# Filling TensorE's waits in a prologue with matmuls that nothing reads

## The chip, the cores and the metric

The kernel runs on one core of one Trainium2 chip. The metric is the device time of one execution in microseconds (us), lower is better. An execution has one launch; the arithmetic is all on the chip.

## The reference

A sliding-window attention is followed by a gated two-layer network. The attention has 8 batches of 576 tokens, 8 heads of 64 dimensions, and each token sees itself and the 63 before it. Its output, 4608 tokens by 512, goes through the network.

```python
scores = (1 / sqrt(64)) * q @ k.T            # rel = i - j, kept where 0 <= rel < 64
attn = softmax(scores) ; x = attn @ v        # x: 4608 x 512
h = x @ w_in                                 # w_in: 512 x 2048
g = h * erf(log(1 + exp(h)))
out = g @ w_out                              # w_out: 2048 x 512, float32
```

The weights arrive as 64-bit floats and have to be brought to the chip's formats by the kernel itself.

## The kernel before

All large products run on TensorE in 16-bit floats, each operand split into a high and a low part, so that a product is three matmuls (high by high, high by low, low by high). Every operand is first scaled by a power of two that its own maximum gives.

The program has two stages that overlap. In the prologue, up to roughly 190 us, the 16 pieces of the 64-bit weights are fetched (L, line 472), turned into 32-bit floats by shifts and masks on VectorE with help of ScalarE and GpSimd (g, d, dd, c, o), and their maxima taken (b, line 508). For each pair of pieces TensorE turns the column of maxima into a row (mb, line 514), VectorE takes its top (mx, line 517), TensorE spreads the top over 128 partitions (my, line 520), and VectorE makes the exponent and the scale from it (mc, lines 305 and 308). ScalarE writes a scaled diagonal (dg, line 529). Then the high part is a scaled copy (h), and the low part is a sum on TensorE: an fp32 matmul of the raw piece with the diagonal, minus the high part (lp, lines 551 and 552), copied out by ScalarE or VectorE (le, line 442 on VectorE). The scales of a chunk of 256 tokens go the same way: row of maxima (pb, line 351), top (px, line 355), spread (py, line 359), copy and scale (pc, line 362).

Attention works on tiles of 128 tokens: scores (s, line 392), masked maximum (m), exponentials on ScalarE, a transposing DMA, weighting of the values (a, line 425), division (n). The network works on chunks of 256 tokens and halves of its 2048 columns: first layer (mm, line 588) into hp, gate on ScalarE and VectorE, second layer (mA and mB, line 624) into o. Attention of later tiles runs beside the network of earlier ones, and after the prologue TensorE has work nearly all the time.

The order of all of it is one long table of words, PLAN (line 47): each word is a step with its arguments, and a loop at the end calls the steps in that order. Each engine executes its own instructions in this order and waits, by semaphores, only for what a step needs. Nothing overtakes on an engine, apart from loads of weights on TensorE.

One tile in TensorE's accumulation memory, av (line 280), holds two banks of 512 columns: the weighted values in the first columns of each, then the rows and columns of the scale steps just described (crow, call, wrow, wall, lines 283 and 284). The columns from 391 on of the first bank are unused. The identity matrix ident (128x128, bf16) is made by GpSimd at the start (line 292).

Of the kernel before, what the change touches and what calls it, by code (L numbers as in the profile page):

```python
# [19 lines left out]
W = 64  # L20
DM, DF = 512, 2048
NT = B * S
P = 128
# [189 lines left out]
def window_attention_gated_ffn(ctx, tc, q, k, v, w_in, w_out, masks, out):  # L213
    nc = tc.nc
# [420 lines left out]
    def store(c, j):  # L635
        r0 = c * CT + j * P
        nc.sync.dma_start(out[r0:r0 + P, :], ob[c % len(ob)][:, j, :])

    def table(n):
        nc.scalar.preload_act_table_set(("exp_and_others", "softplus", "sigmoid_and_others")[n])  # L640

# [64 lines left out]
```

## Time and profile before

| What | Value |
|---|---|
| Median of 3 runs | 949.46 us (947.31 to 952.27) |
| The profiled execution | 949.97 us |
| its span in the profile | 948.2 us |
| TensorE busy (matmuls) | 882.9 us, 93% |
| VectorE, ScalarE, GpSimd busy | 688.1, 639.1, 306.1 us |
| Mean granted clock as recorded | 0.986 |

PE is TensorE's matmuls and PEld its loads of weights, DVE is VectorE, ACT ScalarE, POOL GpSimd, SP the engine that issues the DMAs. A row such as "L551 MATMUL o<-stage,diag x2" names the line of the kernel, the result and the operands. The idle time in brackets is that of the engine just before the row, and behind the arrow stands what ended it. An fp32 matmul shows as two records. A granted clock of 1.00 is 2.4 GHz and 0.50 is 1.2 GHz, its two levels; a value between is a mean over the stretch.

### The profile page before, as it was taken

What the parts mean: (1) busy time and instruction counts of PE and PEld (TensorE: products, weight loads), DVE (VectorE), ACT (ScalarE), POOL (GpSimd) and SP (SyncE); (2) the same over time, 40 slices, a digit from 0 to 9 for tenths busy, and PEclk for the clock granted to TensorE, in tenths of its full rate; (3) what the DMA queues carried; (4) which work ended last, traced back from release to release, by engine and by line L of the source; (5) the groups of instructions that cost most, each with busy time, mean ns of one, the idle gap of its engine ahead of it and who ended that gap; (6) DMA issues with size and microseconds to landing.
All of it is one profiled execution on the core that took longest, in us unless ns stands there. A gap on an engine that the chain in (4) does not pass through costs nothing.

```text
span 948.2 us, 21207 instructions
## 1 busy us (share of the span) xinstructions
PE 882.9 (93%) x8774; PEld 576.7 (61%) x8774; DVE 688.1 (73%) x1531; ACT 639.1 (67%) x739; POOL 306.1 (32%) x270
## 2 busy tenths in 40 slices
PE   0849798899999999999999999999999999999998
PEld 0327466656666666676666666766666666676663
DVE  6889898989889878476868676868686768644232
ACT  4868978789587785384848484848485847574553
POOL 1334243622245441424242424252525252501000
PEclk9979899999999999999999999999999999999999
DMA  9484573433444642343434444443334342301000
GB/s 368 138 212 157 153 173 103 130 100 101 129 107 114 128 118 79 57 112 65 127 77 114 74 117 77 114 78 113 89 103 97 94 92 65 75 17 39 9 23 22
DMA packets 140528, 98.56 MB, mean 104 GB/s; under 512 B 117776, under 2 KB 117904, under 8 KB 140432
## 3 DMA queue, kind: packets, MB, share of 16 engines
q1 hardware_dynamic: 140432, 97.22, 39.9%
q8 instruction: 68, 1.11, 0.5%
q14 instruction: 28, 0.23, 0.1%
HBM read 59.44 MB, written 9.44 MB: 73 GB/s over the span
## 4 chain that ended last, share of the span: by engine, by line
PE 68%; DVE 13%; DMA 8%; ACT 6%; issue 3%; POOL 1%; SPq 0%; DVEq 0%; ACTq 0%; POOLq 0%
PE o L624 36%; PE hp L588 24%; DMA vr<-v_in 4%; PE av L425 3%; DVE vs L320 2%; PE s L392 2%; DVE y L608 2%; PE o L551 2%; DMA stage<-w_in 1%; DMA pt<-p 1%; DVE peaks L341 1%; DMA kr<-k_in 1%; DMA stage<-w_out 1%; DVE ob L633 1%; DVE ks L320 1%
## 5 line engine op out<-in xcount | busy, mean ns | idle before, releaser
L588 PE MATMUL hp<-xt,w 128*128 128x256 f16 x3456 | 393.6, 273 | 3.0 <-ACT h L313 2.2
L588 PEld LDWEIGHTS <-w 128*128 128x128 f16 x3456 | 336.0, 98 | 57.1 <-issue 4.9
L624 PE MATMUL o<-w,gh 128*128 128x512 f16 x1152 | 260.8, 380 | 0.5 <-ACT ob L313 0.3
L624 PEld LDWEIGHTS <-gh 128*128 128x128 f16 x1152 | 109.4, 98 | 124.1 <-issue 0.9
L313 ACT ACTIVATE h<-hp,c 128x512 f32<-128x512 f32 x76 | 51.5, 679 | 137.4 <-PE hp L588 137.3
L624 PE MATMUL o<-w,gl 128*128 128x512 f16 x576 | 136.6, 380 | 0.0
L320 DVE SCALAR_TENSOR_TENSOR gl<-y,sg,gh 128x1024 f16<-128x1024 f32 x72 | 93.1, 1294 | 26.3 <-PE o L624 24.0
L313 ACT ACTIVATE gh<-y,sg 128x1024 f16<-128x1024 f32 x67 | 76.7, 1145 | 49.4 <-DVE y L608 31.0
L415 POOL TENSOR_TENSOR p<-sm,p 128x512 f16<-128x512 f32 x63 | 80.6, 1281 | 62.6 <-ACT sm L411 62.5
L608 DVE TENSOR_TENSOR y<-h,y 128x1024 f32<-128x1024 f32 x72 | 86.5, 1221 | 14.7 <-ACT y L604 14.7
L406 POOL TENSOR_TENSOR sm<-sm,mx 128x512 f32<-128x512 f32 x41 | 46.6, 1139 | 150.1 <-DVE mx L401 150.1
L315 DVE TENSOR_SCALAR h<-hp,c 128x512 f32<-128x512 f32 x68 | 50.4, 744 | 54.5 <-PE hp L588 53.7
L448 POOL TENSOR_TENSOR xs<-x,xs 128x512 f16<-128x512 f32 x33 | 52.2, 1583 | 111.0 <-DVE xs L442 84.2
L624 PEld LDWEIGHTS <-gl 128*128 128x128 f16 x576 | 52.7, 98 | 54.9
L410 ACT ACTIVATE p<-sm,shift,cde 128x512 f16<-128x512 f32 x72 | 58.2, 808 | 36.3 <-POOL sm L406 30.9
L401 DVE CUSTOM_DVE_ANT_0 sm<-s,mask 128x128 f32<-128x128 f32 x288 | 64.9, 285 | 17.7 <-POOL p L415 10.5
L317 POOL TENSOR_SCALAR qs<-qr,csc 128x512 f16<-128x512 f32 x28 | 29.8, 1074 | 148.6 <-DVE csc L308 135.8
L600 ACT ACTIVATE y<-h 128x1024 f32<-128x1024 f32 x72 | 72.9, 1050 | 2.1 <-DVE gl L320 1.5
L604 ACT ACTIVATE y<-y 128x1024 f32<-128x1024 f32 x72 | 73.0, 1050 | 0.4
L411 ACT ACTIVATE sm<-sm,shift,cde 128x512 f32<-128x512 f32 x72 | 58.6, 814 | 2.4
L633 DVE SCALAR_TENSOR_TENSOR ob<-o,sg,ob 128x512 f32<-128x512 f32 x36 | 26.3, 745 | 41.9 <-PE o L624 41.8
L320 DVE SCALAR_TENSOR_TENSOR vs<-vr,csc,vs 128x1024 f16<-128x1024 f32 x36 | 54.0, 1527 | 2.9 <-POOL vs L317 2.9
(142 smaller groups left out, 963.5 us busy)
## 6 DMA issues: line engine op xcount, KB each, us to landing
vr<-v_in SPq DMA_DIRECT2D x36, 512.0 KB, 4.6
kr<-k_in SPq DMA_DIRECT2D x36, 384.0 KB, 3.5
qr<-q_in SPq DMA_DIRECT2D x36, 256.0 KB, 2.7
out<-ob SPq DMA_DIRECT2D x36, 256.0 KB, 2.4
stage<-w_out SPq DMA_DIRECT2D x6, 1024.0 KB, 6.0
stage<-w_in SPq DMA_DIRECT2D x4, 1024.0 KB, 5.5
w<-w_in SPq DMA_DIRECT2D x2, 1024.0 KB, 10.4
w<-w_out SPq DMA_DIRECT2D x2, 1024.0 KB, 6.1
```

What stands on the lines that cost most here:

```text
L313: nc.scalar.activation(dst, src, AF.Copy, scale=s)
L320: nc.vector.scalar_tensor_tensor(dst, src, s, hi, op0=ALU.mult, op1=ALU.subtract)
L401: nc.vector.tensor_tensor_reduce(smi(u, par)[:, j, :], sps[par][:, j, :], mask[:, var, :], 1.0, LOWEST, op0=ALU.add, op1=ALU.max, accum_ou ...
L410: nc.scalar.activation(pp[0][u % 2][:, HP * par:HP * par + HP, :], s, AF.Exp, bias=shift14, scale=es)
L411: nc.scalar.activation(s, s, AF.Exp, bias=shift14, scale=es)
L415: eng_of(eng).tensor_tensor(pp[1][u % 2][:, sl, :], smi(u, par), pp[0][u % 2][:, sl, :], op=ALU.subtract)
L448: eng_of(eng).tensor_tensor(xs[1][u % 2], x_flat(u), xs[0][u % 2], op=ALU.subtract)
L588: nc.tensor.matmul(hps[pc % 2][:, f, :], w1[a][:, cc, fs], xt[b][c % 2][:, cc, :], start=(n == 0), stop=(n == 3 * NCC - 1))
L600: nc.scalar.activation(at(yb, g, n), at(hb, g, n), AF.Softplus)
L604: nc.scalar.activation(y, y, AF.Erf)
L608: nc.vector.tensor_tensor(y, at(hb, g, n), y, op=ALU.mult)
L624: nc.tensor.matmul(ops[j], a[:, f, ts], w2[b][:, hf * GF + f, :], start=f == 0 and a is gh and b == 0, stop=f == GF - 1 and a is gl)
```

## The change

A step wm is added. It multiplies ident by the first 120 columns of ident, n times, into the unused columns of av. Nothing reads that result. PLAN gets 19 such words, all in its first quarter; no other word moves, and the instructions of VectorE, ScalarE, GpSimd and SP stand in the same order as before.

```diff
+    idle = avb[:, 0, row_at + P + 3:row_at + P + 123]
...
+    def warm(k, n):
+        for _ in range(n):
+            nc.tensor.matmul(idle, ident, ident[:, :120], start=True, stop=True)
...
-        "mB": lambda g, n: mm2(g, n, 1), "fo": result, "st": store, "T": table,
+        "mB": lambda g, n: mm2(g, n, 1), "fo": result, "st": store, "T": table, "wm": warm,
...
-    "L:0 L:1 L:2 L:3 lq:0 lk:1 L:4 lm lv:0 lk:0 lq:1 lv:1 L:5 g:0:g d:0 c:0:v g:1:a o:0 d:1 b:0:a c:1:v dd:2 o:1 "
+    "wm:0:207 L:0 L:1 L:2 L:3 lq:0 lk:1 L:4 lm lv:0 lk:0 lq:1 lv:1 L:5 g:0:g d:0 c:0:v g:1:a o:0 d:1 b:0:a c:1:v "
```

The first number of a word counts the blocks, the second is n. In the order of the table, with the TensorE steps around them:

| Block: n | Stands between |
|---|---|
| 0: 207 | start, row of maxima of pair 0 (mb:0) |
| 1: 60 | mb:0, my:0 |
| 2: 14 | my:0, mb:1 |
| 3: 8 | mb:1, first low-part sum (lp:0:1) |
| 4: 8 | lp:0:0, pb:0 |
| 5: 35 | lp:1:0, scores of tile 0 |
| 6: 34 | scores of tile 0, mb:2 |
| 7: 5 | lp:2:0, lp:1:1 |
| 8: 15 | my:2, lp:2:1 |
| 9: 12 | scores of tile 1, lp:4:0 |
| 10: 43 | lp:4:1, weighting of tile 0 |
| 11: 43 | weighting of tile 0, mb:3 |
| 12: 5 | my:3, pb:1 |
| 13: 10 | pb:1, py:1 |
| 14: 15 | py:1, lp:6:0 |
| 15: 5 | lp:6:1, first layer (mm:0:1) |
| 16: 9 | mb:5, my:5 |
| 17: 26 | my:5, lp:10:0 |
| 18: 16 | lp:10:0, lp:10:1 |

TensorE at the start of the program, before: the row of maxima of pair 0 (acc by ident), then the spreading of its top (wtop by ones).

```order
L514 LDWEIGHTS acc [waits Activation_49]
L514 MATMUL av<-ident,acc 1x128
L514 LDWEIGHTS acc [waits Activation_49]
L514 MATMUL av<-ident,acc 1x128
L520 LDWEIGHTS ones
L520 MATMUL av<-wtop,ones 128x1 [waits DVE_49]
```

TensorE at the same place now, three lines further down in the file; each of the 60 filler matmuls of block 1 has its own load of ident.

```order
L517 LDWEIGHTS acc [waits Activation_49]
L517 MATMUL av<-ident,acc 1x128
L644 LDWEIGHTS ident
L644 MATMUL av<-ident 128x120
...
L523 LDWEIGHTS ones
L523 MATMUL av<-wtop,ones 128x1 [waits DVE_49]
L644 LDWEIGHTS ident
L644 MATMUL av<-ident 128x120
```

Block 1 stands between the row of maxima and the spreading of its top, block 2 behind the spreading.

TensorE at the scale of the second chunk, before: row of maxima (cmx), spreading (cdiag by ones), then the low-part sum of piece 6.

```order
L351 LDWEIGHTS cmx [waits DVE_49]
L351 MATMUL av<-ident,cmx 3x128 [waits DVE_49]
L359 LDWEIGHTS ones
L359 MATMUL av<-cdiag,ones 128x3 [waits DVE_49]
L551 MATMUL o_156<-stage_149,diag_89 128x512 [waits DMAHW5_49,DVE_49,Activation_49]
```

And now, with blocks 13 (10 matmuls) and 14 (15) cut to their first pair.

```order
L354 LDWEIGHTS cmx [waits DVE_49]
L354 MATMUL av<-ident,cmx 3x128 [waits DVE_49]
L644 LDWEIGHTS ident
L644 MATMUL av<-ident 128x120
...
L362 LDWEIGHTS ones
L362 MATMUL av<-cdiag,ones 128x3 [waits DVE_49]
L644 LDWEIGHTS ident
L644 MATMUL av<-ident 128x120
...
L554 MATMUL o_156<-stage_149,diag_89 128x512 [waits DMAHW5_49,DVE_49,Activation_49]
```

Block 13 stands between the row of maxima and the step that spreads its top, block 14 between that and the sum.

## Rows read from the trace of the kernel before

**Rows 1.** The page, busy us by engine (share of the span) and instructions.
```profile
PE 882.9 (93%) x8774; PEld 576.7 (61%) x8774; DVE 688.1 (73%) x1531; ACT 639.1 (67%) x739; POOL 306.1 (32%) x270
```

**Rows 2.** The chain of waits, 0 to 110 us: start, us, what.
```profile
23.68 2.08 PE o L551 x2
...
59.23 2.08 PE o L551 x2
...
74.32 0.29 PE o L552
74.61 5.25 PE hp L588 x48
```

**Rows 3.** Stretch, length, busy us of PE, PEld, DVE, ACT, POOL, clock, DMA, GB/s.
```profile
20.00:30.00 10.00, 6.20 (x13) 1.81 (x12) 9.24 (x22) 9.24 (x15) 1.36 (x1) 1.00 0.48 178
```

**Rows 4.** Stretches of four microseconds, the same columns, granted clock third from the end.
```profile
54.00:58.00 4.00, 0.00 (x0) 0.00 (x0) 3.69 (x4) 3.97 (x5) 1.10 (x1) 0.50 0.63 253
...
62.00:66.00 4.00, 3.17 (x52) 1.30 (x50) 2.71 (x6) 1.26 (x3) 0.54 (x2) 0.74 0.84 218
...
70.00:74.00 4.00, 3.86 (x5) 1.46 (x6) 4.00 (x6) 4.00 (x6) 2.90 (x3) 0.50 0.16 33
74.00:78.00 4.00, 4.00 (x35) 3.33 (x34) 3.53 (x4) 2.12 (x4) 0.00 (x0) 0.96 0.65 200
```

**Rows 5.** TensorE in order: start, us, operation, count, idle before and releaser.
```profile
1.80 0.26 PE L514 MATMUL av<-ident,acc 128*1 128x128 bf16 x1 [1.80 <-POOL ident masks.py:199]
...
17.52 0.27 PE L514 MATMUL av<-ident,acc 128*1 128x128 bf16 x1 [4.82 <-ACT stage L508]
...
34.96 0.37 PE L514 MATMUL av<-ident,acc 128*1 128x128 bf16 x2
...
37.74 2.08 PE L551 MATMUL o<-w,diag 128*128 128x512 f32 x2 [0.22 <-ACT w L440]
...
48.18 1.06 PE L551 MATMUL o<-h,diag 128*128 128x512 f32 x2
...
53.29 0.27 PE L514 MATMUL av<-ident,acc 128*1 128x128 bf16 x2
58.75 0.27 PE L514 MATMUL av<-ident,acc 128*1 128x128 bf16 x1 [5.19 <-ACT stage L508]
...
67.37 0.22 PE L351 MATMUL av<-ident,cmx 128*3 128x128 bf16 x1 [1.81 <-DVE x L432]
68.14 0.16 PE L359 MATMUL av<-cdiag,ones 3*128 3x3 bf16 x1 [0.56 <-DVE cdiag L356]
70.14 2.04 PE L551 MATMUL o<-stage,diag 128*128 128x512 f32 x2 [1.84 <-ACT qs L313]
...
95.99 0.22 PE L514 MATMUL av<-ident,acc 128*1 128x128 bf16 x1 [0.61 <-ACT stage L508]
```

**Rows 6.** VectorE in order of time, the same columns.
```profile
21.37 0.27 DVE L517 TENSOR_REDUCE wtop<-av 1x1 bf16<-1x128 f32 x1
21.90 0.16 DVE L305 TENSOR_SCALAR kw<-av 128x1 int32<-128x1 int32 x1 [0.25 <-PE av L520]
...
38.72 0.68 DVE L442 CAST w<-o 128x512 f16<-128x512 f32 x1
...
42.52 0.16 DVE L305 TENSOR_SCALAR kw<-av 128x1 int32<-128x1 int32 x1 [2.34 <-PE av L520]
...
64.54 0.28 DVE L517 TENSOR_REDUCE wtop<-av 1x1 bf16<-1x128 f32 x1 [1.07 <-PE av L425]
...
67.62 0.28 DVE L355 TENSOR_REDUCE ctop<-av 3x1 f32<-3x128 f32 x1 [0.31 <-PE av L351]
...
68.39 0.15 DVE L362 COPY cpw<-av 128x3 f32<-128x3 f32 x1
...
107.89 1.22 DVE L608 TENSOR_TENSOR y<-h,y 128x1024 f32<-128x1024 f32 x1 [1.50 <-ACT y L604]
```

**Rows 7.** Weight loads by form: count | busy us, mean ns | idle before, releaser.
```profile
L588 PEld LDWEIGHTS <-w 128*128 128x128 f16 x3456 | 336.0, 98 | 57.1 <-issue 4.9
```

322 rows, old and new, of the table PLAN are left out of this document.

## The prediction

> **What bounds the kernel now.** I read the page's busy times first, then the chain of waits, then stretches of a few microseconds with their granted clock, then TensorE's and VectorE's instructions in order of time. TensorE is busy for 882.9 of 948.2 us [rows 1], so 65.3 us of idle time is all that exists beside its own work, and it lies almost wholly in the prologue. A shorter prologue moves the whole rest forward; a longer one moves it back.
>
> In the prologue the chain jumps between DMA, ACT, VectorE and TensorE. TensorE's share up to 75 us is 15 pieces of the low-part sums of the weights (lines 551 and 552, the steps lp), first at 23.68 and last at 74.32 us, 18.3 us together [rows 2]. They run at half speed: the fp32 pair takes 2.08 us at 37.74 and 1.06 us at 48.18 [rows 5]. The granted clock reads 1.00 for 20 to 30 us [rows 3] although the sums there take 2.08 us too [rows 2]; the column holds nothing real that early, and the durations say 1.2 GHz until about 47 us. Later the column is right: 0.50 at 54 to 58 and at 70 to 74, back up inside 62 to 66 (2.1 us of the four at half, so at 64.1) and inside 74 to 78 (at 74.3) [rows 4]. The fall at 54 came after a stretch in which TensorE mostly waited (5.19 us before 58.75) [rows 5], the two rises 4.9 us after the dense work from 59.23 [rows 2] and 4.2 us after that from 70.14 [rows 5]. So cold work does stand on the chain, and the change aims at it.
>
> **The change part by part.** It adds 570 matmuls of 120 columns (each with a load of 128x128 weights) in 19 blocks, and moves nothing else. Three things count: how long one takes, whether a block outlasts its gap, and who now waits for a block. The last is not in the diff: the result lies in the tile av, and in the built program the VectorE steps that read other parts of av (the top of a row of maxima, line 517, the exponent, line 305, the chunk's top, line 355, and its copy, line 362) count their wait up to the block that stands between producer and reader.
>
> One filler: two 128-column matmuls take 0.27 us where one takes 0.22, at full clock, and 0.37 against 0.27 at half [rows 5], so the pitch is 0.05 and 0.10 us. Those have one weight column; a load of 128 columns lasts 98 ns [rows 7], which is the upper bound if nothing of it hides. I take 0.055 at full clock and 0.10 at half, near the matmul rows, and keep 0.098 for a rival. The Trainium skill, "TensorE: Matmul & The Clock Gate", section "Back-to-back issue gap", speaks against this value: it gives about 81 ns for a sustained stream of load and matmul pairs at 128 columns. By the rows block 0 ends at 15.2 us, by that figure at 18.6, after the 17.52 us at which its successor is due; what follows is in the second rival.
>
> Block 0 (207): it can start at 1.80, when ident is there. With 4.2 us at half clock (the rise from 70.14), 42 matmuls, and 165 x 0.055 = 9.1 us more, it ends at 15.1. The last matmul of pair 0's row is due at 17.52 [rows 5]: cost 0, hidden by ACT's maximum. Block 1 (60): 17.8 + 3.3 + 0.2 of drain = 21.3, and VectorE's line 517 started at 21.37 in its own order [rows 6]: cost 0, with no slack (at half clock 17.8 + 6.0 + 0.2 = 24.0, cost 2.6). Block 2 (14): line 305 at 21.90 [rows 6] must now wait for it, 14 x 0.055 = 0.8 us; VectorE is busy 9.24 of 10 us here [rows 3], so everything queued behind that wait moves by 0.8.
>
> Blocks 3 to 7 (8, 8, 35, 34, 5) lie beside waits for VectorE and ACT: 0. Block 8 (15) stands before line 305 at 42.52, where VectorE waited 2.34 us for TensorE, and TensorE for two cold sums. This is the first place that could gain. VectorE's copy at 38.72 [rows 6], 0.8 later, ends at 40.2; the second sum, warm, is half of 2.08 + 0.43, 1.26 us, to 41.5; then the pair's product (0.15), block 8 (0.8) and 0.2 of drain: 42.65 against 42.52. Term A is 0: gain, VectorE's lateness and the filler cancel (from -0.4 to +2.6).
>
> Term B, the two sums from 59.23: before them TensorE idles 5.19 us [rows 5], and block 11 (43 x 0.055 = 2.4 us) fills less than half, so about 3 us stay idle, as long as stretches after which the clock fell. VectorE waits only 1.07 us for this work at 64.54 [rows 6], so the gain is 0 to 1.1. I take 0.3.
>
> Term C is a loss on the chain itself. From 65.6 to 69.3 us a scale goes back and forth between VectorE and TensorE in tiny steps, and three blocks now stand inside the exchange. Block 12 (5) holds line 305: 0.3. Block 13 (10) stands between the matmul at 67.37 [rows 5] and its reader at 67.62 [rows 6]: 0.55. Block 14 (15) stands between the matmul that ends at 68.30 [rows 5] and the copy at 68.39 [rows 6]: 0.7. Together 1.55 at full clock, 2.9 at half (30 x 0.10, less 0.1). I take 2.2, between, because the clock here fell and rose inside 62 to 74 [rows 4].
>
> Term D, the two sums from 70.14 to 74.6 [rows 2, 5], on which the hidden layer waits: 4.46 us, half of it, 2.2, if the clock is up. Blocks 12 to 14 make this stretch denser but leave waits of 1.8 us on either side [rows 5]; even odds, so 1.1. Term E, block 15 (5), stands straight before that layer's first matmul: 0.3 (0.5 cold). Term F, blocks 16 to 18 (9, 26, 16) at 96 to 104 us: block 17 holds line 305 for 26 x 0.055 = 1.4 us, and VectorE has 1.50 us of waiting for ACT at 107.89 to absorb it [rows 6]: 0 (1.1 at half clock). ACT sets that stretch, so a warm TensorE gains nothing there.
>
> Sum: A 0 - B 0.3 + C 2.2 - D 1.1 + E 0.3 + F 0 = +1.1 us on 949.97 us of the profiled execution, which lies 0.5 us above the median of the three runs, 949.46. From the median I forecast 950.6. The ends of this case: -0.4 - 1.1 + 1.5 - 2.2 + 0.3 = -1.9, so 947.6; and A 0, B 0, C 2.9, D 0, E 0.5 = +3.4, so 952.9.
>
> **The rivals.** First, it works as it looks: the clock stays at 2.4 GHz from about 6 us on and every cold piece of the chain halves. That is 18.3 / 2 = 9.1 us, less the waits for fillers, 0.8 (block 2) + 0.8 (block 8) + 1.55 (C) + 0.3 (E) = 3.45: -5.7, so 943.8. For it: those pieces are on the chain. Against it: VectorE's waits for TensorE at these places are 2.34 and 1.07 us [rows 6], less than the halves of the sums, and the idle before 58.75 is filled by half.
>
> Second, slower: the blocks outlast their gaps. It decides from a pitch of (21.37 - 0.2 - 17.8) / 60 = 0.056 us on for block 1, and (17.52 - 6.0) / 165 = 0.070 for block 0. At 0.098 [rows 7] block 0 ends at 22.1, block 1 at 28.5 with drain, line 517 is 7.1 late, block 2 adds 1.4; C is 2.9, E 0.5, D gives 1.1 back: +10.8, so 960.3. For it: the weight load is longer than the matmul's columns. Against it: the rows of pairs at 0.05. By the Trainium skill's 81 ns the sum would be 2.6 + 1.1 + 2.4 + 0.4 - 1.1 = +5.4, so 954.9.
>
> Third, it doesn't do what it says: the clock falls in the gaps all the same. Then block 1 costs 2.6, block 2 1.4, C 2.9, E 0.5, F 1.1, 8.5 in all with nothing won; where only about half of the blocks run cold, some +4.5, so 954. For it: the waits that stay unfilled around 56, 66 and 70 us. Against it: the clock rose within 5 us of dense work each time.
>
> **How the numbers follow.** The forecast case 0.60, works as it looks 0.12, falls all the same 0.15, outlasts 0.13. A difference of 0.5%, 4.7 us, is about what a measurement can tell from none. Faster by more (under 944.7): half of the first rival and a little, 0.08. Slower by more (over 954.2): half of the third, most of the second and a little of the forecast case, 0.20. Within: 0.72. The range from 945 to 957 leaves out half of the first rival and the upper half of the second; the likeliest case alone spans 947.6 to 952.9.
>
> **What would show it.** Right or wrong step by step: the pitch of the filler's rows, near 0.055 or near 0.1 us; whether block 0 ends before 17.5 and line 517 of pair 0 starts near 21.4; a VectorE wait of about 1 us before line 305 near 22.7; fp32 pairs of 1.06 instead of 2.08 us before 47 us; granted clock at 54 to 74 us; line 355 and line 362 each about half a microsecond or more behind their matmuls. The forecast fails if the hidden layer's first matmul, at 74.61 before [rows 2], starts more than 3 us earlier or later.

## The result and the profile after

The changed kernel takes 953.64 us, the median of 20 executions (949.41 to 958.71), against 949.65 us for the kernel before in the same comparison (946.91 to 954.00). The ratio is 1.0040, with a 95% interval from 1.0025 to 1.0056: slower by 4.0 us, a difference that is there but below the 0.5% which the prediction counted as no change. The profiled execution took 958.03 us, 4.4 us above its median. Its trace therefore shows more loss (8.0 us at the last matmul) than the kernel has on the whole, and its rows are read for where time goes, not for the total.

The page's first part. Line numbers are 3 higher than before up to the new step warm, whose matmul is line 644.

```profile
PE 911.9 (95%) x9344; PEld 611.2 (64%) x9344; DVE 688.9 (72%) x1531; ACT 639.3 (67%) x739; POOL 305.0 (32%) x270
```

TensorE has the 570 new matmuls, and 29.0 us more of busy time than in [rows 1]. The other engines are within 1.1 us of what they were. So the loss is waiting, or work at half clock.

The chain of waits to 110 us says whose (its shares by line, then some of its pieces: start, us, what):

```profile
by line: PE av L644 16.7%; PE o L554 11.2%; PE hp L591 7.2%; DMA stage<-w_in 6.7%; DMA kr<-k_in 5.8%; DVE stage L505 3.9%; issue 3.9%; DVE w L318 3.7%; PE o L555 2.5%; ACT plane L483 2.5%; DVE w L323 1.9%; DVE h L318 1.8%; ACT sm L414 1.5%;
...
17.82 4.94 PE av L644 x60
...
72.09 1.65 PE av L644 x15
...
102.84 1.51 PE av L644 x26
```

The blocks that were to fill idle time are 16.7% of this chain, and three of them are seen here. VectorE in order of time (start, us, operation, idle before and releaser) shows how they came there:

```profile
22.79 0.28 DVE L520 TENSOR_REDUCE wtop<-av 1x1 bf16<-1x128 f32 x1 [1.24 <-PE av L644]
24.17 0.16 DVE L308 TENSOR_SCALAR kw<-av 128x1 int32<-128x1 int32 x1 [1.10 <-PE av L644]
...
32.24 0.16 DVE L308 TENSOR_SCALAR kw<-av 128x1 int32<-128x1 int32 x1 [1.77 <-PE av L644]
...
46.11 0.16 DVE L308 TENSOR_SCALAR kw<-av 128x1 int32<-128x1 int32 x1 [1.49 <-PE av L644]
66.78 0.28 DVE L520 TENSOR_REDUCE wtop<-av 1x1 bf16<-1x128 f32 x1 [0.44 <-PE av L428]
...
71.41 0.28 DVE L358 TENSOR_REDUCE ctop<-av 3x1 f32<-3x128 f32 x1 [1.49 <-PE av L644]
...
71.81 1.38 DVE L575 TENSOR_SCALAR c<-kw,cpw 128x2 f32<-128x2 f32 x1
...
73.77 0.16 DVE L365 COPY cpw<-av 128x3 f32<-128x3 f32 x1 [0.39 <-PE av L644]
```

The releaser is the filler's line almost every time. Against [rows 6], and for the step of pair 1 (32.24) against this row of the kernel before,

```profile
27.83 0.14 DVE L305 TENSOR_SCALAR kw<-av 128x1 int32<-128x1 int32 x1
```

the same steps (the one on 128x2 elements is not among them) are 1.4, 2.3, 4.4, 3.6, 2.2, 3.8 and 5.4 us late. TensorE in order of time shows what the fillers did for the clock:

```profile
1.80 12.64 PE L644 MATMUL av<-ident 128*128 128x120 bf16 x207 [1.80 <-POOL ident masks.py:199]
...
17.75 5.00 PE L644 MATMUL av<-ident 128*128 128x120 bf16 x60
...
28.89 2.07 PE L554 MATMUL o<-stage,diag 128*128 128x512 f32 x2
...
31.18 1.02 PE L644 MATMUL av<-ident 128*128 128x120 bf16 x8
...
62.14 1.45 PE L554 MATMUL o<-y,diag 128*128 128x512 f32 x2 [0.26 <-ACT w L443]
...
72.02 1.71 PE L644 MATMUL av<-ident 128*128 128x120 bf16 x15
75.00 2.05 PE L554 MATMUL o<-stage,diag 128*128 128x512 f32 x2 [1.27 <-ACT qs L316]
...
79.91 5.42 PE L591 MATMUL hp<-xt,w 128*128 128x256 f16 x48
```

The last row is the hidden layer's first; in the same view of the kernel before it was

```profile
74.44 5.40 PE L588 MATMUL hp<-xt,w 128*128 128x256 f16 x48
```

Block 0 ends at 14.44 us, in time. Block 1 then takes 5.00 us where 60 at full clock take 3.3. The sum at 28.89 is cold, the first at 62.14 half cold, and the last pair, from 75.00, as cold as in [rows 5]. The windows (length, then busy us of PE, PEld, DVE, ACT, POOL, granted clock, DMA share, GB/s) agree:

```profile
18.00:22.00 4.00, 4.00 (x49) 4.00 (x47) 3.54 (x4) 3.66 (x6) 0.00 (x0) 0.57 1.03 415
...
54.00:58.00 4.00, 2.74 (x81) 2.52 (x78) 2.91 (x4) 3.92 (x6) 0.00 (x0) 1.00 1.07 407
...
70.00:74.00 4.00, 3.17 (x27) 2.49 (x26) 2.09 (x7) 0.62 (x2) 2.47 (x2) 0.50 0.39 80
74.00:78.00 4.00, 3.00 (x4) 1.31 (x5) 4.00 (x8) 3.83 (x5) 1.17 (x2) 0.50 0.00 0
```

At 54 to 58 us the clock is now 1.00 (it was 0.50 in [rows 4]), but from 70 to 78 us it is half, which is longer than before (0.50 and then 0.96). The fillers hold the clock in some places and not in others, and readers of av pay for them in both.

### The profile page after: what moved, and what is told of

Its sections match the earlier page's. It is cut to its first block, busy times and chain, and to the rows that moved or that the text cites. A ratio compares the mean times of both kernels' runs of the same rounds, so it can differ in the third digit from the quotient of the medians.

```text
span 956.2 us, 22347 instructions
## 1 busy us (share of the span) xinstructions
PE 911.9 (95%) x9344; PEld 611.2 (64%) x9344; DVE 688.9 (72%) x1531; ACT 639.3 (67%) x739; POOL 305.0 (32%) x270
## 4 chain that ended last, share of the span: by engine, by line
PE 72%; DVE 15%; DMA 8%; ACT 3%; issue 2%; POOL 0%; SPq 0%; DVEq 0%; ACTq 0%
PE o L627 37%; PE hp L591 24%; DMA vr<-v_in 5%; PE av L428 4%; DVE vs L323 3%; PE s L395 2%; DVE y L611 2%; PE av L644 2%; PE o L554 1%; DVE peaks L344 1%; DMA stage<-w_in 1%; DMA stage<-w_out 1%; DVE h L318 1%; DVE ob L636 1%; DVE stage L505 1%
```

## The experiments

In the expectations W is the theory that the loss is VectorE's waits through the tile av. Q is its rival, by which the loss sits with TensorE's own work, whoever reads the tile. Ratios are to the kernel before on the same chip, with 95% intervals; one thousandth is 0.95 us. KEEP in the cuts stands for the numbers that each run has there. Where a run's table was written anew, its line numbers are 31 or 32 lower than in the changed kernel: 612 or 613 is then the filler, 522 or 523 a sum, 276 or 277 the exponent (308), 326 the chunk's top (358).

**Another bank.** Blocks 0 to 15 write into the first-layer tile hps[0], which nothing reads or writes before 70 us; blocks 16 to 18, counts and places stay.

```diff
 def warm(k, n):
+    dst = hps[0].rearrange("p a b -> p (a b)")[:, :120] if k < 16 else idle
     for _ in range(n):
-        nc.tensor.matmul(idle, ident, ident[:, :120], ...)
+        nc.tensor.matmul(dst, ident, ident[:, :120], ...)
```

> The same 19 blocks, but blocks 0 to 15 write into a bank that no engine reads before the first layer; blocks 16 to 18 stay in av. Theory W (the loss comes mostly from VectorE waiting, through the tile av, for fillers and for what stands ahead of them on TensorE): VectorE's line 308 of pair 1 no longer waits for the sum and block 4, lines 358 and 365 of the second chunk no longer wait for blocks 13 and 14, so at 2.4 GHz or below 2.5 of the 4 us come back; ratio to before about 1.001 (0.999 to 1.002). Theory Q (the loss comes from TensorE's own queue, the fillers being ahead of real work whoever reads them): ratio stays about 1.004. Theory I (as it was meant to be: the clock is the larger thing and helps): 0.997 or less.

Measured: 949.68 us, ratio 0.9994 (0.9977 to 1.0012). The same matmuls at the same places cost nothing once nobody reads their tile; 4.6 thousandths, 4.4 us, are gone, which is the whole loss. VectorE in order of time, then two rows of TensorE:

```profile
27.89 0.14 DVE L308 TENSOR_SCALAR kw<-av 128x1 int32<-128x1 int32 x1
...
66.97 0.28 DVE L358 TENSOR_REDUCE ctop<-av 3x1 f32<-3x128 f32 x1 [0.36 <-PE av L354]
```

```profile
73.25 5.40 PE L591 MATMUL hp<-xt,w 128*128 128x256 f16 x48
...
115.01 0.22 PE L354 MATMUL av<-ident,cmx 128*3 128x128 bf16 x1 [1.60 <-DVE cmx L308]
```

The step of pair 1 no longer waits (27.83 before), and line 358 waits for its own matmul alone. The row that line 520 reads and the column of the exponent (line 308) stand in the second bank of av (line 286 of the changed kernel) and the fillers of the change in its first (line 287), and still those steps waited: what counts is the tile, not the bank. With these waits away the whole is a tie. One of Q's kind is left: line 308 of pair 0 waits 1.10 us at 22.70 us for its own spreading matmul, which stands behind block 1 at half clock; the step of pair 1 is on time all the same. In this trace the hidden layer begins 1.2 us ahead of the kernel before (73.25 for 74.44), and the lead is gone at the third chunk's scale (115.01 for 114.92), behind 1.60 us in which TensorE idles.

**Half of the blocks.** First block 0 alone, then block 0 with the blocks behind which nothing on VectorE waits, then with those behind which something does.

```diff
 for tok in PLAN.split():
     name, *args = tok.split(":")
+    if name == "wm" and int(args[0]) not in KEEP: continue
# e2: KEEP = (0,)
# e3: KEEP = (0, 5, 6, 9, 10, 11, 15, 18)
# e4: KEEP = (0, 1, 2, 3, 4, 7, 8, 12, 13, 14, 16, 17)
```

> Only block 0 (207 matmuls) is left. Theory W: nothing waits for it and it ends near 14.4 us, so no loss; the clock is up for the first sums and falls again in the gaps; ratio 1.000 (0.998 to 1.001). Theory Q: 207 of 570 matmuls, all in a gap that hides them; 1.000 too. Theory I: the sums from 23.7 us on run at full speed and VectorE's wait of 2.34 us at 42.5 shrinks; 0.998 or less.

> Blocks 0, 5, 6, 9, 10, 11, 15, 18 are left (395 matmuls), those that no VectorE step waits for; 1 to 4, 7, 8, 12 to 14, 16, 17 (175) are gone. Theory W: the loss is gone, 1.000 (0.998 to 1.001), and the second and fourth sums may run warm. Theory Q: two thirds of the filler matmuls are left, so some two thirds of the loss, 1.0025 (1.002 to 1.004). Theory I: 0.998 or less.

> Block 0 and the blocks that VectorE steps wait for (1 to 4, 7, 8, 12 to 14, 16, 17; 382 matmuls together). Theory W: the whole loss stays, or more, since the gaps between are less filled and the clock falls more often; 1.004 (1.003 to 1.006). Theory Q: the part of the 175, 1.001 to 1.002. Theory I: between e2 and the full change, below 1.0.

Measured: block 0 alone 948.75 us, 0.9977 (0.9965 to 0.9989), a gain of 2 us that its one profile does not locate (it is theory I's number, but not for I's reason: the sum at 23.70 us is cold in it, 2.07 us). The unwaited blocks 952.83 us, 1.0025 (1.0013 to 1.0037), against W, which had no loss here, and what Q said. The waited blocks 951.94 us, 1.0018 (1.0007 to 1.0028), less than W said, and in Q's range. By these two times alone Q would stand; against it are the other bank (0.9994 where Q had 1.004) and the next run. VectorE in the run of the waited blocks:

```profile
28.92 0.14 DVE L308 TENSOR_SCALAR kw<-av 128x1 int32<-128x1 int32 x1
...
45.41 0.16 DVE L308 TENSOR_SCALAR kw<-av 128x1 int32<-128x1 int32 x1 [2.83 <-PE av L644]
```

Pair 1's step does not wait here, because the sum and block 4 ahead of it ran at full clock; the one at 45.41 waits 2.83 us behind a cold sum. So a wait through av costs what stands ahead of it, and how much that is hangs on the clock. The run of the unwaited blocks needed its own trace, TensorE in order of time:

```profile
114.96 0.22 PE L354 MATMUL av<-ident,cmx 128*3 128x128 bf16 x1 [1.75 <-DVE cmx L308]
...
116.86 5.31 PE L627 MATMUL o<-w,gh 128*128 128x512 f16 x16
```

and the kernel before at the same place:

```profile
114.92 0.22 PE L351 MATMUL av<-ident,cmx 128*3 128x128 bf16 x1 [0.37 <-DVE cmx L305]
...
116.82 3.63 PE L624 MATMUL o<-w,gh 128*128 128x512 f16 x16
```

With those blocks the hidden layer begins at 72.64 us, 1.8 us ahead of the 74.44 of the kernel before in the same view. TensorE then has its work done early and idles 1.75 us instead of 0.37 before the third chunk's scale, where the lead is gone (114.96 for 114.92). And the clock falls there: the 16 matmuls of the second layer take 5.31 us instead of 3.63, a loss of 1.7 us in dense work, where no filler stood.

**The gap that the gain opens.** The unwaited blocks again, with one block of 25 put ahead of that scale.

```diff
# PLAN, beside KEEP = (0, 5, 6, 9, 10, 11, 15, 18)
- ... lp:11:0 sp:1:1 ...
+ ... lp:11:0 wm:19:25 sp:1:1 ...
```

> The unwaited blocks of e3 and a block 19 of 25 matmuls ahead of the third chunk's row of maxima. In e3 TensorE came 1.3 us earlier to this place, idled 1.75 instead of 0.37 us and ran the second layer from 116.9 us at half clock, 5.31 instead of 3.63 us. Theory G (e3's loss is the clock's fall there): the loss goes, 0.999 to 1.0005, and the profile shows 3.6 us. Theory Q (filler matmuls in TensorE's queue cost as such): no better than e3, 1.0025 or more.

Measured: 949.94 us, 0.9997 (0.9985 to 1.0009). TensorE at the place:

```profile
114.31 0.22 PE L323 MATMUL av<-ident,cmx 128*3 128x128 bf16 x1 [0.29 <-DVE cmx L277]
...
116.21 3.63 PE L596 MATMUL o<-w,gh 128*128 128x512 f16 x16
```

The 16 matmuls are back at 3.63 us and the loss of the unwaited blocks is gone, with more fillers and not fewer. Q is not needed for it, and had 1.0025 or more.

**One matmul in each block; the three blocks of the chunk's scale.** Both keep block 0 and write to av. The first asks whether a block's length matters or what stands ahead of it; the second takes term C alone.

```diff
# e7: wm:1 to wm:18 each with one matmul (wm:1:60 -> wm:1:1, ...)
# e8: KEEP = (0, 12, 13, 14)
```

> Block 0 with 207, every other block with one matmul, in av: VectorE waits as in the full change, but nearly without the fillers' length. Theory W with length: 0.1 us for each of the eleven waits and the wait of pair 1's line 308 for the sum ahead of block 4, about 1 us; against e2 (0.9977) some +0.001, so 0.998 to 1.000. If the wait for what stands ahead of the blocks is the larger part, not the length: 1.002 to 1.004.

> Block 0 and the three blocks inside the second chunk's exchange (12, 13, 14: 30 matmuls, in av). This is the forecast's term C alone: 1.55 us at 2.4 GHz, 2.9 at 1.2, against e2. The clock there is mostly down when the gaps before are unfilled, so about +2.5 us: 1.0005 (0.9995 to 1.0015). If ScalarE's chain after 84 us hides it: 0.998 as in e2.

Measured: one matmul each 952.44 us, 1.0022 (1.0010 to 1.0035); the three blocks 954.84 us, 1.0039 (1.0019 to 1.0059). VectorE of the first, then of the second:

```profile
28.55 0.16 DVE L277 TENSOR_SCALAR kw<-av 128x1 int32<-128x1 int32 x1 [1.12 <-PE av L613]
```

```profile
69.42 1.37 DVE L575 TENSOR_SCALAR c<-kw,cpw 128x2 f32<-128x2 f32 x1
```

One matmul (0.21 us in the trace) makes the step of pair 1 wait 1.12 us, for the sum ahead of it. That agrees with the second of the two expectations. It is not a clean comparison, though: without the full blocks the clock is half from 31.4 to 41.7 and from 51.9 to 65.6 us in that profile, so part of the 4.3 us against block 0 alone can be the clock. The three blocks cost 5.9 us against block 0 alone, where some 2.5 were expected: a miss. In their profile the hidden layer begins at 77.01 us, 1.1 us later than with block 0 alone (75.90) and 2.6 later than before; the rest is open.

**Filled to the end, and read by nobody.** Blocks 0 to 14 in hps[0]; the short ones made as long as their gaps; blocks 15 to 18 gone; the block at 113 us added. Then three variants of it: more gaps filled, the blocks 10 to 14 taken out, and all blocks in av.

```diff
 def warm(k, n):
+    dst = hps[0].rearrange("p a b -> p (a b)")[:, :120] if k < 16 else idle
# PLAN: wm:0:207 -> 245, wm:4:8 -> 16, wm:7:5 -> 22, wm:11:43 -> 86,
#       wm:12:5 -> 25, wm:13:10 -> 8, wm:14:15 -> 27,
#       wm:15 to wm:18 taken out, wm:19:25 behind lp:11:0
# e6: also wm:22:50 behind my:5, wm:23:6 behind mx:6,
#     wm:24:13 behind xt:4:1 (into the score banks)
# e5b: wm:10 to wm:14 taken out
# e5_in_av: dst = idle for all
```

> What the change was after, without what it paid for it: blocks 0 to 14 write into the bank that nobody reads before the first layer, with more matmuls where TensorE still idled (block 0 245, 4 16, 7 22, 11 86, 12 25, 13 8, 14 27), blocks 15 to 18 are gone, and a block 19 of 25 stands ahead of the third chunk's row of maxima, where TensorE idled about 1.7 us at 113 us. Theory W with the clock as a second term (waits cost, and the clock's falls in the gaps and at 117 us take the gain back): 0.997 (0.994 to 0.999). Theory W alone (the clock is worth nothing, since ScalarE and VectorE set the pace of the prologue): 0.999 to 1.001.

> e5 and three blocks in score banks that nobody reads at that time: 50 matmuls after the spreading of pair 5's top (TensorE idled 3.3 us there, and the clock was down from 95 to 102 us), 6 and 13 around 148 us, ahead of a first-layer stretch that ran 7.07 instead of 5.4 us in e5. If every fall of the clock on the chain costs: 0.9945 (0.993 to 0.996). If ScalarE hides the first place and the fall at 150 us comes anyway: as e5, 0.996.

> e5 without blocks 10 to 14, so that TensorE idles from 49 to 58 us and around 64 to 68 us as before the change. Forecast terms B and D alone: if a held clock there is worth up to 1.1 + 2.2 us, the time goes up by 2 to 3 us against e5, to 0.998 to 0.9995. If other engines set the pace of that stretch: 0.996 as e5.

> e5 with every block back in av, so that VectorE waits for blocks 1 to 4, 7, 8 and 12 to 14 again (the same matmuls, the same gaps). Theory W: the waits at 2.4 GHz, 0.8 (block 2) + about 1 (block 4 and the sum ahead of it) + 1.0 (block 7, 22) + 0.8 (block 8) + 1.2 + 0.45 + 1.4 (12 to 14), some 4 to 6 us lost: 1.000 to 1.003. If the fillers' result tile does not matter: 0.996.

| Kernel | us | ratio to before (95%) |
|---|---|---|
| filled, other bank | 945.78 | 0.9961 (0.9944 to 0.9979) |
| with more gaps | 947.94 | 0.9967 (0.9955 to 0.9979) |
| without blocks 10 to 14 | 950.59 | 1.0000 (0.9989 to 1.0011) |
| filled, all in av | 953.28 | 1.0032 (1.0017 to 1.0046) |

The filled version beats both kernels, by 3.7 us and by about 7.5. Its TensorE in order of time, and one of its windows:

```profile
1.81 15.15 PE L613 MATMUL hp<-ident 128*128 128x120 bf16 x245 [1.81 <-POOL ident masks.py:199]
17.49 3.33 PE L613 MATMUL hp<-ident 128*128 128x120 bf16 x60
...
52.50 4.69 PE L613 MATMUL hp<-ident 128*128 128x120 bf16 x86
...
67.81 1.14 PE L522 MATMUL o<-stage,diag 128*128 128x512 f32 x2 [0.33 <-ACT qs L284]
...
70.11 5.49 PE L559 MATMUL hp<-xt,w 128*128 128x256 f16 x48
```

```profile
70.00:74.00 4.00, 4.00 (x37) 3.33 (x35) 4.00 (x6) 2.99 (x5) 0.67 (x1) 1.00 0.69 231
```

Block 0 lasts until 16.96 us, and the 60 matmuls of block 1 take 3.33 us, not 5.00. The clock stays up to 95.0 us, the sums before the hidden layer take 1.14 instead of 2.04, and that layer starts at 70.11 instead of 74.44. Without blocks 10 to 14 the same rows are cold again:

```profile
57.10 2.08 PE L522 MATMUL o<-y,diag 128*128 128x512 f32 x2 [0.21 <-ACT w L411]
...
68.85 2.05 PE L522 MATMUL o<-stage,diag 128*128 128x512 f32 x2 [3.02 <-ACT qs L284]
...
73.25 6.11 PE L559 MATMUL hp<-xt,w 128*128 128x256 f16 x48
```

3.9 thousandths, 3.7 us, are what these five blocks bring, the difference of two comparisons of which each is known to 1 or 2 us. (The filled version was timed on another chip than its three variants; the kernel before took 949.92 us on the one and 950.32 on the other.) With all blocks in av the clock is up to 101.3 us as well, but VectorE reads:

```profile
65.54 0.16 DVE L276 TENSOR_SCALAR kw<-av 128x1 int32<-128x1 int32 x1 [1.62 <-PE av L612]
...
68.10 0.28 DVE L326 TENSOR_REDUCE ctop<-av 3x1 f32<-3x128 f32 x1 [0.84 <-PE av L612]
```

Seven such waits from 20 to 74 us sum to 6.4 us, against 1.5 us in four waits for av in the version with the other bank. The tile alone makes 7.1 thousandths, 6.7 us, and turns the best version into a loss. More gaps (the first variant) brought nothing. Behind my:5 ScalarE set the pace: the sum there starts at 97.17 us, with 97.06 in the filled version, although it now runs at full clock. Done earlier, TensorE then idles 1.81 us for ScalarE, and the 24 matmuls of the hidden layer at 105.67 us take 4.33 us, with 2.78 in the filled version; and the clock fell at 149.8 us all the same.

## Why the prediction was right in its answer and short in its sum

**The answer.** No change beyond 0.5% was forecast, +1.1 us, and +4.0 us was measured. That is inside the range, 0.7 us above the likeliest case's own end of 952.9. The two mechanisms named were the ones at work: readers of av wait for fillers, and the clock is not held where much of a gap stays idle. The first is shown (the other bank takes the loss away; the tile av brings it back in the filled version), and so is the second (longer blocks hold the clock). But there was luck in the answer: 4.0 us is close below the 4.7 that would have been a change. And the number nearest to the measured one is not the forecast case's 950.6 but the third rival's (the clock falls in the gaps all the same, about half of the blocks cold: +4.5, so 954), which had a chance of 0.15. The trace looks like it: block 1, the sum at 28.89, blocks 13 and 14 and the sums from 75.00 are cold, the sums from 42 to 52 us are not. The rival's own terms are not what happened either: it priced block 1 at 2.6 and gave nothing to blocks 3 to 7.

**A reading that was wrong.** The fall of the clock at 54 us in the kernel before was put down to the 5.19 us of waiting ahead of 58.75. That wait begins at 53.56 us, and the clock fell at 53.9 (it reads 0.93 from 53 to 54 us and 0.50 behind that): nearly all of the wait came after the fall, and ahead of it TensorE had idled 0.79 and 1.95 us. So term B's word on idle time "as long as stretches after which the clock fell" does not rest on this place.

**The pitch.** 0.055 us at full clock and 0.10 at half were right: 3.33 / 60 = 0.056 and 4.69 / 86 = 0.055 in the filled version, 1.71 / 15 = 0.11 with its drain where the clock was half. So the rival "the blocks outlast their gaps", which needed 0.098, is refuted. The Trainium skill, "TensorE: Matmul & The Clock Gate", section "Back-to-back issue gap", has about 81 ns for such a stream at 128 columns; the 0.055 us measured here at 120 columns decide against it.

**Block 0, block 1, block 2.** Block 0: 14.44 for 15.1 us, cost 0 as said. Block 1: "cost 0, with no slack (at half clock ... cost 2.6)". There was no slack, and the clock did fall, 0.75 us into the block, so line 520 came 1.4 us late. What failed is the assumption that the clock survives the gap from 14.64 to 17.60 us. With block 0 up to 16.96 it does; and it did in the run of the waited blocks, where the same 207 matmuls took 13.58 us, 1.91 us stayed idle and block 1 took 3.37 us, so this miss of 1.4 us can differ from one execution to the next. Block 2: 0.8 forecast, 2.27 - 1.42 = 0.85 measured.

**"Blocks 3 to 7 lie beside waits for VectorE and ACT: 0."** This step failed, and it is the largest miss. Line 308 of pair 1, free at 30.47 us, waits until 32.24. Its column was ready at 28.96, but the wait counted up to block 4, and TensorE had a cold sum (28.89 to 31.39) and block 4 to do first. The step is 4.41 us late after 2.27: 2.1 us. The prediction had found that waits count up to the block, and did not apply it to this one, since it looked at the blocks' own length; what has to be counted is everything that stands between the producer and the block. It is not a fixed price: with the sum at full clock the wait was 0 (the waited blocks) or 0.69 us (filled, all in av).

**Terms A to F, in the profiled execution.** A: the step is 3.6 us late where 0.1 was forecast, all of it carried over from blocks 1 to 4 less 0.8 regained. B, a gain of 0.3 by the forecast and 1.1 at most: from that lateness to line 520 at 66.78, 2.24 late, 1.35 us come back, 0.67 of it from the first sum to line 520 (66.78 - 62.14 = 4.64 for 64.54 - 59.23 = 5.31) and the other half before it. C: from line 520 to the first sum before the hidden layer 75.00 - 66.78 = 8.22 us, before 70.14 - 64.54 = 5.60: +2.6, with 2.2 taken and 2.9 as the end at half clock. D: 0, where even odds gave -1.1; the sums are as cold as before. E: with D's stretch 79.91 - 75.00 = 4.91 for 4.30, +0.6, forecast 0.3 and 0.5 cold. By the hidden layer's first matmul this is 1.4 + 0.85 + 2.1 - 0.8 - 1.35 + 2.6 + 0.6 = +5.5 us (79.91 - 74.44), more than the 3 us that the forecast allowed in either direction; that test of it failed, in this execution.

F: block 17 makes line 308 wait 1.15 us, forecast 1.4 or less, and hidden. On ScalarE it is hidden (its table load of 105.51 us comes at 111.03, 5.5 us late as the hidden layer is, and VectorE's wait of 1.50 us there is gone). But VectorE is also the one that frees the buffer of v: the next fetch of v is issued at 113.57 instead of 107.08 us, and the step that takes its maxima waits for it, as it did not before. VectorE, then TensorE of the changed kernel:

```profile
120.65 0.69 DVE L344 TENSOR_REDUCE peaks<-vr 128x1 f32<-128x512 f32 x1 [1.89 <-DMA vr<-v_in]
```

```profile
121.80 0.22 PE L354 MATMUL av<-ident,cmx 128*3 128x128 bf16 x1 [1.73 <-DVE cmx L308]
```

The third chunk's scale is thus 121.80 - 114.92 = 6.9 us late, 1.4 more than the hidden layer. Not all of that is the block's: a step on few elements behind it took longer too (line 580 at 110.12 us, 1.12 us for 0.28 before). The forecast looked for this wait at ScalarE alone.

**What was undervalued.** The gain. B and D were given 1.4 us together, 3.3 at most; fully held, and in a bank that nobody reads, blocks 10 to 14 are worth 3.7 us. The reason given for doubt, that the waits stay half unfilled, was right for this change and is no limit of the method: 86 matmuls in place of 43 fill the stretch. The rival "it works as it looks", 943.8 us, is what the filled version comes near (945.78), with three edits that the change lacks: another bank, longer blocks, and one at 113 us. Without the first it is a loss; the other two were not taken out of it one by one.

**What stays open.** Why block 0 alone gains 2 us, and why three blocks beside it cost 5.9 us. From a chunk's scale near 200 us (line 351) to the last group of the second layer the profiled executions differ by up to 4.6 us (739.4 with the waited blocks, 744.0 with the three blocks, 740.3 before), where no filler stands in any of them, so one profile of each does not tell.

## What to carry to other kernels

A filler costs its length only on its own engine; for everybody else it costs all that stands ahead of it, if it writes into a tile that they read, so let it write into a tile that nobody reads then. Whether it held the clock hung here on what stayed idle behind it: behind the same 43 matmuls the next sum took 1.17 us where 1.34 us stayed idle and 1.45 us where 2.21 did, so a block that leaves much of its gap open can pay without buying. A stretch that becomes faster opens a new gap behind it: look there for a clock that now falls, before concluding that the gain was not real.

## What the runs showed of the hardware

TensorE's granted clock went from full to half at 18.5 us in the changed kernel, in the middle of back-to-back matmuls, after 12.64 us of dense work, 2.96 us of idle time and the first 0.75 us of block 1, and came back at 21.9. I had expected a gap of that size to be harmless after so much work. In the other-bank run the same came of 2.83 us (block 1 took 4.95 us). With 0.18 us idle (the filled version) it did not fall, nor with 1.91 us (the waited blocks).

Block 11, of 43 matmuls, is alike. TensorE with the unwaited blocks, then in the changed kernel:

```profile
56.31 0.22 PE L517 MATMUL av<-ident,acc 128*1 128x128 bf16 x1 [1.34 <-ACT stage L511]
56.79 1.17 PE L554 MATMUL o<-y,diag 128*128 128x512 f32 x2 [0.26 <-ACT w L443]
```

```profile
61.66 0.22 PE L517 MATMUL av<-ident,acc 128*1 128x128 bf16 x1 [2.21 <-ACT stage L511]
```

Behind the second of these the sum is half cold (1.45 us at 62.14), and so is that of the other-bank run (1.55 us, behind 2.78 us); with 86 matmuls 0.21 us stays idle. The length of the idle time is not all: inside 1.44 us of it, at 66.6 us, the clock fell in the other-bank run too, with five fillers ahead. Each kernel has one trace here, and no run gives a limit.

A VectorE step on 128x2 elements took 1.38 us at 71.81 us, and 1.37 us in the run with three blocks. It took 0.21 in the trace before; that row, and GpSimd in the changed kernel at the time of the step:

```profile
68.02 0.21 DVE L572 TENSOR_SCALAR c<-kw,cpw 128x2 f32<-128x2 f32 x1
```

```profile
71.83 1.34 POOL L481 TENSOR_SCALAR plane<-w 128x1024 f16<-128x1024 f32 x1
```

The two end within 0.02 us of each other (73.19 and 73.17), as if VectorE had been held for GpSimd's whole instruction. The other-bank run has it again (67.36 to 68.55 us, a GpSimd instruction from 67.38 to 68.53), while in the trace before the step started 0.06 us ahead of GpSimd's and was short. In the changed kernel it cost nothing, because block 14 (72.02 to 73.73) held the copy at 73.77 longer still. Without that cover it does: in the other-bank run the copy starts 1.35 us behind the start of this step (68.71), before 0.37 us (68.39). The Trainium skill, "SBUF — State Buffer", section "Who interferes with whom", says that the two engines share a pair of ports to the on-chip memory, and that where VectorE works in a mode that uses the pair, the one that has it keeps the other out for a whole instruction. The coincidence agrees with that as far as the holding goes; by the rows VectorE's step starts 0.02 us ahead of GpSimd's, and no run here tests which of the two is first.
